# A hand-placed order of 820 operations replaced by another order of the same operations

## The chip, the cores and the metric

The kernel runs on one core of one Trainium2 chip. The time is the device time of one execution in microseconds; the median of three timed runs before the change is 188.65 us (188.63 to 188.68). One more execution was taken with the hardware profiler.

## What is computed

Two layers over 2048 steps and 640 channels, written side by side into one output of 2048 x 1280.

Half A is a diagonal state space layer with 640 complex states: `Bu = x B_bar^T`, then `h_t = Lam_bar h_{t-1} + Bu_t`, then `y = 2 Re(h C^T) + x * Dskip`, where `Lam_bar = exp(dt * Lam)` and `B_bar = (Lam_bar - 1)/Lam * B`.

Half B is a gated long convolution: `k` is convolved along time with four taps per channel, `kv = k_shift * v`, then `y = causal convolution of kv with a kernel of 2048 taps per channel + kv * ssm_D`, and the output is `q * y`. The reference does the long convolution by a Fourier transform of length 4096.

## The kernel before

The kernel is written as a list of operations. Each `P.add(name, engines, function, outs, ins, group)` appends one operation and gives it the next number; there are 820. `depend` works out from the memory that operations read and write which must come first. A group is a use of PSUM banks: its first operation (the products on TensorE) waits until the last user of those banks is done, and its last operation (the eviction) frees them.

Nothing is scheduled by a planner when the kernel is built. A string, `ORDER`, gives one token for each operation, such as `794T0`: the operation's number, its engine (V VectorE, A ScalarE, G GpSimd, T TensorE, S the SP queue for DMAs; a DMA can be issued on A too), and the first PSUM bank of its group (of eight). A small `t` is TensorE with the product cut in two column halves. `emit` walks through the string and issues each operation on the engine it names. So every engine runs its operations strictly in the string's order, the SP queue issues its DMAs strictly in that order, and the string also decides which engine does an operation that several can do, and which bank a product uses.

How the work is staged, in the order of time:

- Warm-up products, sine tables made by GpSimd (`wqh`, `gqh`, `sph`) and ScalarE (`w_s`, `g_s`), and a long chain of small VectorE operations on the 640 parameters (from `t_par`, `pv` to `fi`). B is loaded, turned on TensorE (`turn_B`) and evicted (`ev_B`).
- Half A upwards: `up2`, `up1`, `up0` join steps into blocks of 2, 4, 8 and 16 (line 588 holds the products with x, line 226 the others); `x` comes in eight transposing loads (`ld_x0` to `ld_x7`, line 554). Then `coarse` runs the recurrence over 128 blocks (`cs_...`), `gC` builds the output matrix, and `dn3` to `dn0` spread the states back to single steps (`ad`, line 735, adds on VectorE).
- Half B in two halves of 320 channels (`hf` 0 and 1): `s1h`, `s2h` transform the kernel, `conv` applies the four taps to five blocks of 128 channels (`cm`, `ca`, `cx`; line 832 loads k and v, and the k tile has one buffer), `plane` and `relay` re-arrange kv through DRAM, `s1k`, `s2k` transform kv, `product` multiplies the spectra (`pp`, `pq`, `py`, `pz`), `r2` and `r1` transform back (line 969 and 990 the products, 974 and 1008 or 1006 the evictions), `em1` multiplies by q when the eviction was done by ScalarE, and `store` writes.
- The output of half A, `project(i)` for 16 row sets: `ld_r` loads x rows (line 743, four buffers in turn), `xd` multiplies them by Dskip (line 744), `C` is the product (line 226 or 230), `ev_C` adds the two on VectorE (line 770) or only copies on ScalarE (line 768), in which case `em_C` adds (line 776), and `st_A` stores (line 780). Row set 13 is split into two halves, `C13_0` and `C13_1`, each with one bank; the others use two.

Numbers that matter below: 163, 162 and 168, 169 `ld_Braw`; 92 `t_par`, 93 `pv`, 109 `fi`; 170, 172 `turn_B1` and 171, 173 `ev_B1`; 220 `up21_0`, the first product with x, 222, 223 `up21_2` and its eviction; 177 `ld_x0`; 379, 390, 401, 445, 456 the five k loads; 195 and 209 the evictions `e1h0_2`, `e1h0_9`; 200 `s1h0_5`; 237 `ev_up0c_0`; 316 `r16`; 91 `ld_Dr` (Dskip to all partitions); 727, 728 `C0`, `ev_C0`; 732 `C1`; 744 `st_A3`; 504 `s2k0_30`, 505 `e2k0_30`; 699, 700 `r11_0`, `er11_0`; 702, 703 `r11_6`, `er11_6`; 705, 706 `r11_12`, `er11_12`; 720 `em11_28`; 708 to 711 and 721 to 724 the stores of half B's second half; 770, 771 `C8`, `ev_C8`; 808 `ld_r14`; 792 `ld_r12`, 793 `xd12`, 794 `C12`, 795 `ev_C12`; 809 `xd14`, 811 `ev_C14`; 816 `C15`, 817 `ev_C15`; 800, 801 `C13_0`, `ev_C13_0`; 804, 805 `C13_1`, `ev_C13_1`; 803, 807 their stores.

The loop that turns the string into instructions, and the place where it is read:

```python
for i, e, bank in order:
    o = self.ops[i]
    ...
    own = range(bank, bank + o.group.nb)
    if o is o.group.ops[0]:
        need |= {held[b] for b in own if held[b] is not None}
...
order = [(int(x[:-2]), x[-2].upper(), int(x[-1])) for x in ORDER.split()] if ORDER else plain_order(c.P)
c.P.narrow = {int(x[:-2]) for x in ORDER.split() if x[-2] == "t"}
```

Of the kernel before, what the change touches and what calls it, by code (L numbers as in the profile page):

```python
# [1115 lines left out]
def plain_order(P):  # L1116
# [19 lines left out]
    "169A0 157G0 162S0 0V0 58G0 6T0 17G0 168A0 163S0 110G0 19V0 148G0 87V0 11G0 18V0 89A0 90S0 12G0 3T1 42G0 13V0 88S0 183S0 "  # L1136
    "67G0 22V0 4T0 25V0 172T1 26G0 23V0 65V0 149G0 39V0 66V0 112G0 59V0 72G0 9T0 184S0 166T2 46G0 30G0 170T0 69G0 181S0 92T3 "
    "5T4 93V3 20V0 10T5 111G0 94A0 68G0 167A2 95V0 1T4 164T5 32V0 161G0 2T4 182S0 125V0 123V0 102V0 165A5 31V0 128V0 96V0 8T2 "
    "103V0 21V0 104V0 61V0 173A1 7T4 127V0 105V0 28V0 14V0 106V0 220T2 60V0 101A0 107V0 100A0 36V0 98A0 108V0 171A0 124V0 37V0 "
    "174S0 38V0 129V0 33V0 109V0 40V0 62V0 114G0 318V0 113G0 126V0 27V0 115G0 29V0 41V0 116G0 117G0 150G0 222T0 221A2 175S0 "  # L1140
    "118G0 43G0 97A0 99A0 119A0 44G0 212T2 156S0 63A0 121V0 152G0 379S0 71A0 223V0 15A0 47G0 70A0 210T0 213V2 153G0 45A0 120V0 "
    "50G0 122V0 179S0 214T2 132V0 144V0 211A0 52G0 147V0 160A0 188S0 74G0 180S0 218T0 130V0 382A0 51G0 131V0 48G0 34A0 228T4 "
    "381A0 77G0 187S0 186S0 54G0 215A2 383V0 216T6 73G0 219A0 133V0 158S0 384A0 229V4 82G0 238T0 83G0 185S0 134V0 217A6 35V0 "
    "55G0 135V0 49A0 380S0 262T6 385V0 56G0 386A0 78G0 254T4 79G0 53A0 387V0 390S0 151G0 75A0 226T2 263V6 239A0 177S0 255A4 "
    "84G0 189V0 57A0 178S0 388V0 202T4 155A0 196T6 246T0 203V4 197A6 391S0 392V0 227A2 393V0 137V0 394V0 192T2 247A0 230T6 "
    "270S0 193A2 395V0 396V0 76A0 154A0 224T2 397V0 145V0 231A6 401S0 136V0 146V0 142A0 64V0 204T0 398V0 225A2 190T6 240T4 81A0 "
    "399V0 389S0 402S0 205A0 141A0 191A6 200T0 404V0 194t2 16A0 139A0 232T6 138V0 24V0 195A2 403V0 272S0 405V0 143A0 201A0 80A0 "
    "406V0 198T0 407V0 241A4 248T2 199A0 408V0 400S0 233A6 409V0 86A0 445S0 242T4 249A2 316V0 206T0 243A4 250T2 140A0 207A0 "
    "410V0 234T6 412S0 251A2 244T4 208T0 235A6 176V0 245A4 411S0 252T2 236T6 256T4 253A2 416S0 209A0 237A6 85A0 321V0 159S0 "
    "317V0 448V0 302T6 447V0 257A4 314T0 303A6 319t2 258T4 320V2 315A0 310T6 449V0 415S0 259A4 312T2 311A6 417S0 260T4 300T0 "  # L1150
    "414S0 322V0 261A4 450V0 304T6 313A2 413S0 264T4 323V0 305A6 273S0 301A0 451V0 306T0 418S0 452V0 265A4 324t6 419S0 298T2 "
    "307A0 325V6 266T4 446S0 299A2 274T0 267V4 282T6 326V0 268T4 275A0 286T2 283V6 269A4 308T0 287A2 327V0 328t6 296T4 330V0 "
    "309A0 276T2 329V6 297A4 294T0 277V2 725S0 424t6 456S0 295A0 331V0 280T4 337T2 332V0 281A4 432T0 425A6 335V0 333T4 338A2 "
    "278T6 334V4 271S0 433A0 288T2 279V6 434T4 289A2 336V0 426T0 730S0 453V0 435A4 339t6 441S0 442S0 420T2 427A0 340V6 422T4 "
# [93 lines left out]
```

## Time and profile before

| | us |
|---|---|
| median of three runs (188.63 to 188.68) | 188.65 |
| the profiled execution | 187.94 |
| its span, first to last instruction | 186.2 |
| TensorE busy | 175.9 (94%) |
| VectorE busy | 157.2 (84%) |
| ScalarE busy | 147.4 (79%) |
| GpSimd busy | 72.1 (39%) |

Times in the profile count from the span's start. In a row of a timeline the first number is the start, the second how long it took, then the engine, the line of the kernel, the operation, what it writes and reads, the shapes, the number of instructions merged into the row, and in brackets how long the engine sat idle before and what ended that. `SPq` rows are the time that the SP queue took to issue a DMA, not the transfer. In the table of stretches, each engine's busy time is followed by its number of instructions, then come the granted TensorE clock, the mean busy share of the DMA engines and GB/s. In a row of a group the numbers after the bar are busy us and the mean of one in ns, after the second bar the idle time before. Matmuls are pipelined and their ends are modelled, so neighbouring rows overlap a little.

### The profile page before, as it was taken

The numbers are of one execution on the slowest core, as the hardware profiler recorded it, in microseconds if no ns is written. First come the engines' busy times: TensorE is split into PE (matmuls) and PEld (weight loads), VectorE is DVE, ScalarE is ACT, GpSimd is POOL, SyncE is SP. The second block draws the span as 40 slices with busy tenths as digits, with TensorE's granted clock in tenths as the row PEclk, the third lists the DMA queues.
The fourth block names the chain that finished last, engine by engine and source line by source line (L and its number), as shares of the span: only waits on it lengthen the run. The fifth ranks groups of instructions, "written<-read, shape, count | busy, mean of one in ns | idle before, by whom it ended". The sixth has DMA issues, their size and how long they took to land.

```text
span 186.2 us, 7668 instructions
## 1 busy us (share of the span) xinstructions
PE 175.9 (94%) x3398; PEld 121.9 (65%) x3399; DVE 157.2 (84%) x227; ACT 147.4 (79%) x181; POOL 72.1 (39%) x68
## 2 busy tenths in 40 slices
PE   7999999999999989889989999999999999999991
PEld 3554555455668766566676588776578876887770
DVE  3538767799659899999979989899999999998971
ACT  2369797999999999999997988997898874984000
POOL 8669999900000000016804924820830000541620
PEclk9999999999999999999999999999999999999999
DMA  5999999899999989999999579302496993058995
GB/s 156 189 180 166 202 152 129 165 171 212 192 239 248 232 145 161 181 167 145 141 108 273 182 151 132 49 5 75 142 186 129 223 209 76 25 158 189 230 212 154
DMA packets 106826, 30.15 MB, mean 162 GB/s; under 512 B 101290, under 2 KB 106154, under 8 KB 106794
## 3 DMA queue, kind: packets, MB, share of 16 engines
q1 hardware_dynamic: 106476, 29.35, 87.5%
q8 instruction: 26, 0.43, 1.1%
q10 hardware_dynamic: 318, 0.33, 0.6%
q14 instruction: 6, 0.05, 0.1%
HBM read 11.32 MB, written 7.86 MB: 103 GB/s over the span
## 4 chain that ended last, share of the span: by engine, by line
PE 39%; DVE 20%; DMA 13%; POOL 11%; SPq 7%; ACT 5%; issue 3%; DVEq 0%; POOLq 0%; ACTq 0%
PE acc L226 17%; DMA arena<-in_B_k_dram 6%; PE acc L918 6%; PE acc L230 5%; SPq L825 4%; DVE arena L206 4%; DVE arena L735 4%; POOL arena L310 4%; PE acc L969 3%; DMA arena<-in_A_Dskip_dram 3%; DMA arena<-in_B_ssm_k_dram 3%; PE acc L990 3%; DVE arena L858 3%; ACT arena L931 2%; ACT arena L974 2%
## 5 line engine op out<-in xcount | busy, mean ns | idle before, releaser
L588 PE MATMUL acc<-arena 128*64 128x512 bf16 x400 | 45.4, 380 | 0.5 <-DVE arena L605 0.3
L931 ACT CAST arena<-acc 128x960 bf16<-128x960 f32 (+1 forms) x43 | 37.4, 916 | 4.0 <-PE acc L918 2.1
L226 PE MATMUL acc<-arena 128*128 128x320 bf16 (+2 forms) x255 | 36.4, 298 | 2.2 <-DVE arena L770 1.0
L904 ACT CAST arena<-acc 128x1024 bf16<-128x1024 f32 x37 | 35.8, 1037 | 1.2 <-PE acc L899 1.2
L588 PEld LDWEIGHTS <-arena 128*64 128x64 bf16 x400 | 22.2, 110 | 20.1 <-DVE arena L605 0.8
L226 PEld LDWEIGHTS <-arena 128*128 128x128 bf16 x256 | 23.7, 98 | 12.0 <-DVE arena L770 1.2
L859 POOL TENSOR_TENSOR arena<-arena 128x2048 bf16<-128x2048 bf16 x2 | 8.5, 4274 | 53.0 <-DVE arena L858 45.2
L918 PE MATMUL acc<-arena 128*64 128x160 bf16 x512 | 23.6, 235 | 1.0 <-DVE arena L686 0.6
L230 PE MATMUL acc<-arena 128*64 128x320 bf16 (+3 forms) x258 | 23.2, 313 | 0.7 <-DVE arena L697 0.5
L918 PEld LDWEIGHTS <-arena 128*64 128x64 bf16 x512 | 18.6, 110 | 7.6 <-ACT arena L931 2.2
L858 DVE TENSOR_TENSOR arena<-arena 128x2048 bf16<-128x2048 bf16 x14 | 17.8, 1269 | 4.7 <-ACT arena L207 4.5
L735 DVE TENSOR_TENSOR arena<-acc,arena 128x1024 bf16<-128x1024 f32 (+2 forms) x19 | 20.4, 1115 | 0.9 <-PE acc L230 0.5
L776 POOL TENSOR_TENSOR arena<-arena 128x640 bf16<-128x640 f32 x3 | 4.2, 1417 | 32.6 <-ACT arena L768 32.6
L974 ACT CAST arena<-acc 128x1024 bf16<-128x1024 f32 x16 | 15.4, 1026 | 1.7 <-PE acc L969 1.5
L230 PEld LDWEIGHTS <-arena 128*64 128x64 bf16 x258 | 12.9, 110 | 3.8 <-DVE arena L697 0.6
L206 DVE TENSOR_SCALAR arena<-arena 128x2048 bf16<-128x2048 bf16 x15 | 11.0, 749 | 4.9 <-DMA arena<-in_B_k_dram 4.7
L894 PE MATMUL acc<-arena 128*64 128x128 bf16 x400 | 14.6, 221 | 0.5 <-ACT arena L605 0.3
L894 PEld LDWEIGHTS <-arena 128*64 128x64 bf16 x400 | 12.5, 110 | 3.4 <-ACT arena L904 0.9
L770 DVE TENSOR_TENSOR arena<-acc,arena 128x640 bf16<-128x640 f32 (+1 forms) x14 | 10.8, 774 | 3.0 <-PE acc L226 2.5
L207 ACT ACTIVATE arena<-arena 128x2048 bf16<-128x2048 bf16 (+2 forms) x10 | 11.1, 1111 | 1.9 <-DVE arena L858 1.1
L942 DVE TENSOR_TENSOR arena<-arena 128x2560 bf16<-128x2560 bf16 x8 | 11.9, 1485 | 0.1
L609 PE MATMUL acc<-arena 128*64 128x256 bf16 (+2 forms) x140 | 11.4, 291 | 0.2 <-ACT arena L655 0.2
(142 smaller groups left out, 283.0 us busy)
## 6 DMA issues: line engine op xcount, KB each, us to landing
out_dram<-arena SPq DMA_DIRECT2D x31, 160.0 KB, 3.4
arena<-in_B_ssm_k_dram SPq DMA_DIRECT2D x8, 320.0 KB, 5.9
kv_rows<-arena SPq DMA_DIRECT2D x5, 512.0 KB, 4.5
arena<-kv_rows SPq DMA_DIRECT2D x16, 160.0 KB, 4.0
arena<-in_A_x_dram SPq DMA_DIRECT2D x16, 160.0 KB, 3.4
arena<-in_B_q_dram SPq DMA_DIRECT2D x8, 320.0 KB, 6.1
arena<-in_A_B_im_dram ACTq DMA_DIRECT2D x1, 160.0 KB, 3.0
arena<-in_A_B_re_dram SPq DMA_DIRECT2D x1, 160.0 KB, 2.8
```

Source lines behind the costliest of these rows:

```text
L206: vm = lambda e: lambda out, in_, by: e.tensor_scalar_mul(out=out, in0=in_, scalar1=by)
L226: e.matmul(out, lhsT=lhsT, rhs=rhs, start=start, stop=stop, skip_group_check=True)
L230: e.matmul(out[half], lhsT=lhsT[:, half], rhs=rhs, start=start, stop=stop, skip_group_check=True, tile_position=(0, 64 * r))
L588: e.matmul(o[64 * r:64 * r + 64], lhsT=self.BT[j][:, r, d, :], rhs=self.XP[:, d, 2 * q:2 * q + 2], start=(d == 0), stop=(d == 4), skip_gro ...
L735: e.tensor_tensor(out=o, in0=b, in1=o, op=ALU.add)
L858: P.add(f"ca{d}_{j}", tt, lambda e: e.tensor_tensor(out=t1, in0=t1, in1=t2, op=ALU.add), outs=[t1], ins=[t1, t2])
L894: e.matmul(B[64 * b:64 * b + 64, 128 * i:128 * i + 128], lhsT=lh[i], rhs=F[:, b, :], start=True, stop=True, tile_position=(0, 64 * b))
L904: P.add(f"e1{what}{hf}_{u}", {PACT: act(1024), PDVE: dve(1024)}, lambda e, B: c.CP[e](out=out, in_=(B.rearrange("p (l n s k) -> p k s l n" ...
L918: e.matmul(B[64 * s:64 * s + 64, 512 * b + 160 * i:512 * b + 160 * i + 160], lhsT=c.W[:, k, 64 * b:64 * b + 64], rhs=self.AS[hf][:, k, 160 ...
L931: c.CP[e](out=out, in_=b.rearrange("p r (k j n) -> p r k j n", k=n, j=4) if nj > 1 else b.rearrange("p r (k x) -> p r k x", k=n))
L942: P.add(f"pp{hf}", n1, lambda e: e.tensor_tensor(out=pt, in0=X, in1=Yk, op=ALU.mult), outs=[pt], ins=[X, Yk])
L974: P.add(f"er2{hf}_{u}", {PACT: act(1024), PDVE: dve(1024)}, lambda e, B: c.CP[e](out=out, in_=B.rearrange("p (s n b) -> p b s n", s=2, n=4 ...
```

## The change

Only the string `ORDER` changes. It has the same 820 numbers; the functions, the shapes and the number of products cut in halves (40) stay. Tokens move, 61 of them name another engine, and many name another bank. Of the operations that can run on several engines, VectorE has 242 tokens instead of 231, ScalarE 173 instead of 182, GpSimd 72 instead of 74. (An `em` token makes no instruction when its eviction is on VectorE.) The lines that are spoken of below:

```diff
 ORDER = (
...
-    "67G0 22V0 4T0 25V0 172T1 26G0 23V0 65V0 149G0 39V0 66V0 112G0 59V0 72G0 9T0 184S0 166T2 46G0 30G0 170T0 69G0 181S0 92T3 "
-    "5T4 93V3 20V0 10T5 111G0 94A0 68G0 167A2 95V0 1T4 164T5 32V0 161G0 2T4 182S0 125V0 123V0 102V0 165A5 31V0 128V0 96V0 8T2 "
-    "103V0 21V0 104V0 61V0 173A1 7T4 127V0 105V0 28V0 14V0 106V0 220T2 60V0 101A0 107V0 100A0 36V0 98A0 108V0 171A0 124V0 37V0 "
...
-    "118G0 43G0 97A0 99A0 119A0 44G0 212T2 156S0 63A0 121V0 152G0 379S0 71A0 223V0 15A0 47G0 70A0 210T0 213V2 153G0 45A0 120V0 "
...
-    "55G0 135V0 49A0 380S0 262T6 385V0 56G0 386A0 78G0 254T4 79G0 53A0 387V0 390S0 151G0 75A0 226T2 263V6 239A0 177S0 255A4 "
...
-    "439A2 459V0 440S0 345t6 458V0 352A4 284T0 502T2 346V6 460G0 285A0 349t4 503A2 91S0 467T0 350V4 353t6 468A0 292T2 354V6 "
...
-    "569V0 769V0 571S0 699T0 771V6 772V0 705T2 700A0 702T4 773S0 712T6 572S0 701V0 810T0 713A6 579S0 706V2 707G0 570S0 573S0 "
-    "714G0 703V4 704G0 815V0 708S0 816T4 792S0 809G0 709S0 799V0 710S0 811V0 812G0 718T2 715T6 793G0 813S0 719V2 720V0 794T0 "
-    "711S0 716V6 717G0 817V4 818V0 723S0 721S0 724S0 800T4 795V0 796G0 819S0 722S0 797S0 804T0 801V4 802G0 803S0 805V0 806G0 "
-    "807S0"
...
+    "112G0 61V0 26G0 22V0 21V0 67G0 126V0 10T1 46G0 183S0 166T0 72G0 92T1 7T2 93V1 128V0 94A0 113G0 125V0 15A0 30G0 95V0 157G0 "
+    "127V0 172T1 28V0 102V0 181S0 96V0 103V0 39V0 98A0 164T2 124V0 97A0 38V0 65V0 100A0 101A0 104V0 6T3 167A0 105V0 37V0 106V0 "
+    "36V0 3T4 107V0 14V0 165A2 108V0 109V0 9T0 32V0 40V0 114G0 66V0 182S0 99A0 41V0 111G0 1T4 59V0 115G0 60V0 110G0 25V0 173V1 "
+    "69G0 4T0 129V0 170T1 220T4 31V0 116G0 171V1 73G0 175S0 130V0 68G0 62V0 117G0 222T0 131V0 149G0 221V4 118G0 174S0 148G0 "
+    "47G0 27V0 150G0 212T4 156S0 48G0 379S0 54G0 49A0 210T2 56G0 119A0 121V0 152G0 120V0 177S0 42G0 218T6 33V0 211A2 29V0 44G0 "
+    "213V4 223A0 179S0 55G0 160V0 63A0 228T0 34A0 82G0 382A0 35V0 144V0 180S0 74G0 122V0 224T4 70A0 151G0 229V0 185S0 188S0 "
...
+    "241A4 134V0 204T6 195V0 316G0 242T4 205A6 202T2 403V0 81A0 200T0 404V0 232T6 201A0 402S0 405V0 203A2 406V0 80A0 407V0 "
+    "248T2 85A0 389S0 408V0 137V0 409V0 243A4 445S0 233A6 208T0 249A2 317V0 244T4 136V0 234T6 209V0 245A4 138A0 143A0 139A0 "
+    "250T2 235A6 140A0 410V0 141A0 206T4 251A2 236T6 252T2 207A4 256T0 413S0 237V6 142V0 411S0 176V0 253A2 86A0 91S0 321V0 "
...
+    "680A6 798S0 573S0 577S0 718T6 771V0 772G0 702T4 799G0 719A6 705T2 773S0 699T0 578S0 810T6 700V0 701G0 579S0 580S0 706V2 "
+    "707V0 808S0 720V0 703V4 704V0 712T2 715T0 815V0 708S0 794T4 716V0 717G0 710S0 792S0 709S0 713V2 714G0 809G0 722S0 816T2 "
+    "711S0 723S0 793V0 724S0 795V4 796V0 811V6 812V0 797S0 800T4 817V2 818V0 813S0 721S0 804T2 801V4 802V0 803S0 819S0 805V2 "
+    "806V0 807S0"
 )
```

59 rows, old and new, of the table ORDER are left out of this document.

## The prediction

> **What bounds the kernel now.** I read the page first (shares, slices), then a table of busy time in six stretches, then the timelines of TensorE, VectorE, the SP queue and GpSimd at the places where the new list differs. The one profiled execution took 187.94 us, 1.74 more than its span, and lies 0.71 under the median 188.65 of the three timed runs; differences are worked out inside the span and added to that median.
>
> ```profile
> span 186.2 us, 7668 instructions
> PE 175.9 (94%) x3398; PEld 121.9 (65%) x3399; DVE 157.2 (84%) x227; ACT 147.4 (79%) x181; POOL 72.1 (39%) x68
> ```
>
> ```profile
> core 0: us, PE busy (x) PEld busy (x) DVE busy (x) ACT busy (x) POOL busy (x), PEclk, DMA share, GB/s
> 0.00:9.46 9.46, 8.39 (x42) 4.07 (x43) 4.51 (x34) 3.27 (x6) 7.00 (x23) 1.00 0.83 174
> 9.46:37.40 27.94, 27.57 (x253) 14.13 (x252) 19.46 (x37) 23.94 (x31) 26.50 (x28) 1.00 1.19 166
> 37.40:66.30 28.90, 27.67 (x454) 19.00 (x455) 23.85 (x33) 27.93 (x41) 0.28 (x1) 1.00 1.10 217
> 66.30:98.10 31.80, 29.04 (x725) 20.98 (x726) 30.13 (x39) 31.08 (x38) 8.14 (x2) 1.00 1.04 144
> 98.10:165.90 67.80, 66.72 (x1573) 51.75 (x1574) 65.34 (x72) 57.36 (x66) 25.16 (x12) 1.00 0.65 133
> 165.90:182.40 16.50, 16.49 (x358) 11.94 (x356) 13.39 (x17) 3.84 (x4) 4.99 (x3) 1.00 0.89 211
> ```
>
> TensorE sets the pace. Between its first real product at 9.46 and its last at 182.4 it is idle 5.45 us (0.37, 1.23, 2.76, 1.08, 0.01). Both lists hold the same products in nearly the same sequence and as many narrow ones (40), so TensorE's own work does not change; a new order can win at most those 5.45 us, and can lose any amount. Half of it lies between 66.3 and 98.1, where VectorE (30.13 of 31.80) and ScalarE (31.08) are both full, and there the wins must be found. The DMA share is at 1.0 until 98: until then a transfer that moves up pushes others back.
>
> **The front, up to 66 us.** Three edits matter.
>
> ```profile
> 9.46 6.67 PE L588 MATMUL acc<-arena 128*64 128x512 bf16 x60
> 16.46 3.86 PE L588 MATMUL acc<-arena 128*64 128x512 bf16 x34 [0.34 <-DVE arena L605]
> 6.50 0.19 DVE L379 COPY arena<-acc 128x30 f32<-128x30 f32 x1 [3.13 <-PE acc L377]
> 10.18 0.17 DVE L399 CAST arena<-arena 128x10 int32<-128x10 f32 x1
> ```
>
> (1) Eviction 173 (ev_B1) goes from ScalarE to VectorE, into bank 1 and behind the whole chain of small parameter operations, which in the kernel before runs from 6.50 (pv) to the end of 10.18 (fi), 3.8 us. The last turn (170) needs that bank and stands directly ahead of the first product (220). t_par moves up past one turn, so the chain starts about 1.2 us earlier, at 5.3, and has 20 operations where it had 27 (0.1 each by the spacing of these rows): fi ends near 8.4. Eight more small ones, 0.8 of eviction (128x640 from PSUM, the row 97.26 below) and the turn's 0.4 give 10.1 to 10.4, less what the chain's own waits may save. I take 10.1: +0.6, bounds -0.1 and +1.4. (2) Eviction 223 leaves VectorE for ScalarE, which takes away the 0.34 before 16.46. Left over: +0.3.
>
> ```profile
> 34.53 2.11 SPq L832 DMA_TRANSPOSE arena<-in_B_k_dram  x1
> 36.68 3.50 SPq L554 DMA_TRANSPOSE arena<-in_A_x_dram  x2
> 46.69 2.18 SPq L832 DMA_TRANSPOSE arena<-in_B_k_dram  x1
> 39.82 1.40 DVE L206 TENSOR_SCALAR arena<-arena 128x2048 bf16<-128x2048 bf16 x2
> ```
>
> (3) On the SP queue ld_x0 (half of the 3.50, 1.75) moves from behind the second k load to ahead of ld_x2. Everything between moves back 1.75: k1 is issued at 36.3, its first taps start at 41.5 instead of 39.82, and VectorE's conv 1 ends as much later. Behind conv 1 on VectorE now stands eviction 195 (e1h0_2, moved there from ScalarE), and the product s1h0_5 (200) waits for the bank that it frees: TensorE is up to 1.2 us late near 52, and all later products queue behind that wait. The third k load is not moved, since x0 has been issued by then: 46.69, or at most 0.4 later.
>
> **From 53 to the product C1 at 98.** What is late there is VectorE, not TensorE.
>
> ```profile
> 53.39 0.75 DVE L206 TENSOR_SCALAR arena<-arena 128x2048 bf16<-128x2048 bf16 x1 [4.00 <-DMA arena<-in_B_k_dram]
> 60.21 0.82 DVE L673 COPY arena<-arena 128x1280 f32<-128x1280 f32 x1
> 95.09 0.53 DVE L827 TENSOR_TENSOR arena<-arena 128x80 bf16<-128x80 bf16 x1 [0.21 <-DMA arena<-in_B_ssm_k_dram]
> 96.64 0.49 DVE L744 TENSOR_TENSOR arena<-arena 128x640 bf16<-128x640 bf16 x1 [1.02 <-DMA arena<-in_A_Dskip_dram]
> 97.26 0.82 DVE L770 TENSOR_TENSOR arena<-acc,arena 128x640 bf16<-128x640 f32 x1
> 53.39:98.09 44.70, 41.18 (x935) 30.42 (x932) 42.12 (x56) 43.52 (x59) 8.14 (x2) 1.00 1.04 169
> 98.14 0.58 PE L226 MATMUL acc<-arena 128*128 128x320 bf16 x3 [0.88 <-DVE arena L770]
> ```
>
> From the landing of the third k to the end of ev_C0 (98.08) VectorE works 42.12 of 44.70 us, and C1 starts when it is done. So what TensorE loses ahead of this, up to about 1 us, is absorbed and counts 0; it is priced as 1.5 in rival (c). In this stretch the new list adds to VectorE e1h0_9 (1.22, a 1024-column eviction as in the row 166.06 below) and an ev_up0c (about 0.4), takes r16 (0.82, to GpSimd, which has nothing else there) and a cf (0.16): +0.6. The Dskip load (ld_Dr) goes up past all the relay loads and the h loads, so the 1.02 before 96.64 goes: -1.0, but the next limits stand close behind: TensorE's own work up to C0, and ScalarE (43.52 of 44.70), which must now also do e2k0_30 (8/12 of the 0.98 below) before C1: +0.4. Sum 0 at C1, bounds -1.2 and +1.2.
>
> **98 to 166.** TensorE is idle 1.08 in 67.8.
>
> ```profile
> 166.06 1.22 DVE L974 CAST arena<-acc 128x1024 bf16<-128x1024 f32 x1
> L974 ACT CAST arena<-acc 128x1024 bf16<-128x1024 f32 x16 | 15.4, 1026 | 1.7 <-PE acc L969 1.5
> L931 ACT CAST arena<-acc 128x960 bf16<-128x960 f32 x33 | 31.1, 978 | 2.0 <-ACT arena L931 0.9 <-PE acc L918 0.3 <-DVE arena L744 0.3
> ```
>
> VectorE gives up three er21 (3.7), ev_C9 and a pz0 (0.8 each), two em10 (1.1) and three xd (1.4), and takes two er21 (2.4), ev_C5, ev_C11 and em_C10 (0.8 each), er10_0 (1.15) and one xd (0.5): 7.8 against 6.5, 1.3 less. ScalarE takes the three er21 (1.03 each) and ev_C9 (0.7) and gives up two er21, two ev_C and er10_0: 0.6 less. Two pq0 change places between VectorE and GpSimd one for one. Three relay loads now stand behind st_A3, which waits for ev_C3 near 112.3; they are issued by 115, when the last one is in the kernel before, so s1k1 is not late. I take -0.2, bounds -1.1 and +1.0.
>
> **The end.** Here I see a new wait.
>
> ```profile
> 168.86 0.82 DVE L770 TENSOR_TENSOR arena<-acc,arena 128x640 bf16<-128x640 f32 x1 [0.21 <-PE acc L226]
> 168.70 1.77 PE L990 MATMUL acc<-arena 64*64 64x80 bf16 x176
> 170.94 1.88 DVE L1008 TENSOR_TENSOR arena<-acc,arena 128x640 bf16<-128x640 f32 x2
> 165.66 0.48 DVE L1013 TENSOR_TENSOR arena<-arena 128x640 bf16<-128x640 bf16 x1
> 172.73 1.21 SPq L1024 DMA_DIRECT2D out_dram<-arena  x2
> 174.04 0.47 SPq L743 DMA_DIRECT2D arena<-in_A_x_dram  x1
> 178.11 1.39 POOL L744 TENSOR_TENSOR arena<-arena 128x640 bf16<-128x640 bf16 x1 [2.95 <-DMA arena<-in_A_x_dram]
> 173.82 1.68 DVE L744 TENSOR_TENSOR arena<-arena 128x640 bf16<-128x640 bf16 x1
> 173.51 1.65 POOL L744 TENSOR_TENSOR arena<-arena 128x640 bf16<-128x640 bf16 x1
> 179.78 0.82 DVE L770 TENSOR_TENSOR arena<-acc,arena 128x640 bf16<-128x640 f32 x1 [0.69 <-PE acc L226]
> 181.07 0.49 DVE L770 TENSOR_TENSOR arena<-acc,arena 128x320 bf16<-128x320 f32 x1 [0.46 <-PE acc L226]
> 182.43 0.49 DVE L770 TENSOR_TENSOR arena<-acc,arena 128x320 bf16<-128x320 f32 x1 [0.87 <-PE acc L226]
> arena<-in_A_x_dram SPq DMA_DIRECT2D x16, 160.0 KB, 3.4
> ```
>
> ld_r12 (792) is issued at 174.04 and xd12 can start 4.07 later, at 178.11; that is 0.3 in time for ev_C12 at 179.78, and nobody waits, since C13_0 takes the banks of C15, not of C12. In the new list ld_r12 stands behind stores 708 and 710, and 708 waits for er11_6, on VectorE behind er11_0 (moved there from ScalarE), er11_12 and em11_28. er11_0's product is now the last of four: done at 168.70 + 1.77 = 170.5. Then VectorE has er11_0 (1.15), er11_12 and er11_6 (the 1.88 of row 170.94 together) and em11_28 (0.48): 3.5 in all, and er11_6 ends at 174.0. Two stores at 0.6 and ld_r12 is issued at 175.2, +1.2. With the 3.4 that such loads have in the median it lands at 178.6, with its own 4.07 at 179.3. xd12 is now on VectorE (0.48), so ev_C12 ends at 179.9 to 180.6; in the kernel before it ends at 180.6 (179.78 + 0.82). But in the new list C13_0 takes bank 4, C12's own, and C13_1 takes bank 2, C15's; on VectorE ev_C14 and ev_C15 are queued behind the waiting xd12 and ev_C12, 0.74 each, so C13_1 may start at 181.4 to 182.1. In the kernel before the rows 181.07 and 182.43, 1.36 apart, put its start at about 181.0. So +0.4 to +1.1 from the load alone; two stores go out just ahead of it, so I take the upper part, +1.0, bounds 0 (landing within 3.0) and +1.8. The last store follows after that as in the kernel before.
>
> The two rows at 173.5 show VectorE's xd13 at 1.68 while GpSimd's xd14 ran 1.65; alone it takes 0.48. [...]
>
> **Sum.** What the front loses (+0.3, and up to +1.2 at the bank of e1h0_2) is absorbed between 53 and 98 and counts 0; the stretch up to C1 counts 0; the stretch 98 to 166 counts -0.2; the end counts +1.0. That is +0.8 in all: 188.65 + 0.8 = 189.45, said as 189.5.
>
> **Rivals.** (a) The load of Dskip is what the new order is worth: the 1.02 and the 0.21 ahead of C1 go, ScalarE has room after all, and ld_r12 lands within 3.0 us: -1.2, 187.4. For it: the rows 96.64 and 98.14 name that load alone; against it: VectorE's +0.6 and the full ScalarE. It decides from the point where ev_C0 is ready before C0 ends. (b) Same operations, same time: the idle is only moved about, the load is in time: 188.65. For it: the 5.45 us are spread over dozens of small bank waits. (c) The front is not absorbed: the 1.75 of conv 1 also holds up the third k load by its single buffer, and 1.5 reach C1 on top of the end's 1.0: 191.0. Against it: 46.69 leaves 1.4 after the last tap in the kernel before.
>
> **Chances.** Forecast 0.43, (a) 0.30, (b) 0.17, (c) 0.10. The measurement tells 0.2% (0.38 us) from nothing; a few hundredths of the forecast fall into that band, and about as many of (b) to the fast side: slower 0.50, same 0.18, faster 0.32. The cases (a) and (c) are the ends of the range, 187.3 to 191.0; the forecast's own range is 188.9 to 190.3.
>
> **What would show it.** The first L588 product at 10.1 (9.4 to 10.9). C1's first L226 product within 1 us of 98.1 with no Dskip wait on VectorE. At the end a VectorE wait at L744 for in_A_x_dram of about 3 us, released near 179, and a TensorE gap at L226 of 0.4 to 1.2 released by VectorE L770. If that L744 operation waits for nothing, or if C1 comes at 97 or sooner, the prediction is wrong.

## The result: slower, and by more than forecast

| | median, us | runs | lowest to highest |
|---|---|---|---|
| kernel before | 188.63 | 7 | 187.21 to 189.22 |
| kernel after | 191.68 | 7 | 189.83 to 194.75 |

The ratio is 1.0148, with a 95% interval of 1.0108 to 1.0187: 2.8 us slower (2.0 to 3.5). The forecast was +0.8 us, in a range that ended at 191.0. The sign was right; the time lies outside the range. The ratios here leave disturbed executions out, which the lowest and highest times hold.

The profiled execution of the kernel after took 192.18 us with a span of 190.4, where that of the kernel before had 186.2. So 4.2 us have to be found in this pair of traces, more than the 2.8 of the medians. One execution is not the median, and what differs from one execution to the next comes out below.

### The profile page after: what moved, and what is told of

The parts are those of the page before. It is cut to its first block, busy times and chain, and to the rows that moved or that the text cites. A ratio compares the mean times of both kernels' runs of the same rounds, so it can differ in the third digit from the quotient of the medians.

```text
span 190.4 us, 7669 instructions
## 1 busy us (share of the span) xinstructions
PE 176.2 (93%) x3396; PEld 121.2 (64%) x3396; DVE 160.5 (84%) x231; ACT 140.2 (74%) x172; POOL 75.6 (40%) x70
## 4 chain that ended last, share of the span: by engine, by line
PE 40%; DVE 20%; SPq 17%; ACT 8%; DMA 6%; issue 6%; POOL 0%; DVEq 0%; ACTq 0%; POOLq 0%
PE acc L226 16%; PE acc L918 7%; DVE arena L735 7%; PE acc L230 7%; SPq L554 6%; DMA arena<-in_B_k_dram 6%; SPq L825 4%; DVE arena L858 3%; ACT arena L904 3%; DVE arena L206 3%; PE acc L969 3%; PE acc L990 3%; SPq L832 3%; SPq L519 3%; PE acc L588 2%
## 5 line engine op out<-in xcount | busy, mean ns | idle before, releaser
L588 PE MATMUL acc<-arena 128*64 128x512 bf16 x400 | 44.9, 379 | 0.0
L230 PE MATMUL acc<-arena 128*64 128x320 bf16 (+2 forms) x252 | 23.3, 318 | 0.1
L770 DVE TENSOR_TENSOR arena<-acc,arena 128x640 bf16<-128x640 f32 (+1 forms) x15 | 11.5, 777 | 4.7 <-PE acc L226 4.0
L744 POOL TENSOR_TENSOR arena<-arena 128x640 bf16<-128x640 bf16 x7 | 9.8, 1400 | 13.5 <-DMA arena<-in_A_x_dram 13.5
L206 DVE TENSOR_SCALAR arena<-arena 128x2048 bf16<-128x2048 bf16 (+1 forms) x17 | 12.4, 750 | 2.4 <-DMA arena<-in_B_k_dram 2.2
L969 PE MATMUL acc<-arena 64*128 64x128 bf16 x320 | 11.4, 224 | 1.1 <-issue 1.1
L1013 POOL TENSOR_TENSOR arena<-arena 128x640 bf16<-128x640 bf16 (+1 forms) x2 | 3.4, 1722 | 22.3 <-ACT arena L1006 22.3
```

The costliest lines, as they stand in the source:

```text
L206: vm = lambda e: lambda out, in_, by: e.tensor_scalar_mul(out=out, in0=in_, scalar1=by)
L230: e.matmul(out[half], lhsT=lhsT[:, half], rhs=rhs, start=start, stop=stop, skip_group_check=True, tile_position=(0, 64 * r))
L588: e.matmul(o[64 * r:64 * r + 64], lhsT=self.BT[j][:, r, d, :], rhs=self.XP[:, d, 2 * q:2 * q + 2], start=(d == 0), stop=(d == 4), skip_gro ...
L969: e.matmul(B[:, 512 * s + 128 * i:512 * s + 128 * i + 128], lhsT=lh[i][s][r], rhs=rh, start=(r == 0), stop=(r == 1), tile_position=(64 * s ...
```

## The profile after

First the page of the kernel after: its first lines, and the shares of the chain that ended last (the kernel before had "issue 3%" there).

```profile
span 190.4 us, 7669 instructions
PE 176.2 (93%) x3396; PEld 121.2 (64%) x3396; DVE 160.5 (84%) x231; ACT 140.2 (74%) x172; POOL 75.6 (40%) x70
...
PE 40%; DVE 20%; SPq 17%; ACT 8%; DMA 6%; issue 6%; POOL 0%; DVEq 0%; ACTq 0%; POOLq 0%
```

TensorE works nearly as long as before (176.2 against 175.9), so nearly all of the loss is idle time. The same six stretches of the kernel after show where it lies:

```profile
0.00:9.46 9.46, 7.16 (x36) 2.90 (x36) 5.06 (x41) 4.26 (x11) 5.92 (x23) 1.00 0.83 167
9.46:37.40 27.94, 27.52 (x257) 14.46 (x259) 20.48 (x29) 19.94 (x21) 26.97 (x29) 1.00 1.14 172
37.40:66.30 28.90, 26.66 (x436) 18.04 (x434) 26.23 (x37) 23.96 (x35) 1.55 (x1) 1.00 1.10 209
66.30:98.10 31.80, 30.10 (x659) 21.33 (x653) 30.38 (x40) 31.13 (x40) 9.48 (x3) 1.00 1.07 161
98.10:165.90 67.80, 65.26 (x1606) 50.27 (x1602) 63.93 (x70) 56.17 (x64) 28.88 (x13) 1.00 0.59 124
165.90:182.40 16.50, 15.04 (x396) 11.50 (x393) 10.69 (x14) 4.76 (x6) 2.79 (x2) 1.00 0.68 169
```

TensorE's idle time, stretch minus its busy time, before and after: 0.37 and 0.42; 1.23 and 2.24; 2.76 and 1.70; 1.08 and 2.54; 0.01 and 1.46. The middle moved as foreseen: one lost near 52, one won back ahead of 98. The last two stretches, in which I had expected -0.2 and, at one place near the end, +1.0, lost 2.9.

The waits of TensorE name what the page calls "issue", time in which the engine waited for nothing that the profile shows. The columns are line, what was waited for, us in total, how often, and the longest:

```profile
PE acc L990 <- issue: 1.4, 3, 1.0
...
PE acc L969 <- issue: 1.1, 1, 1.1
```

A third row of this kind, of 0.98 at line 377 (`t_par`, at 5.59), lies in the warm-up ahead of a product's only instruction; it isn't one of those meant here and comes up again under the front. The kernel before has no such row for TensorE. The timeline of the kernel after shows the four one by one:

```profile
162.14 0.79 PE L990 MATMUL acc<-arena 64*64 64x80 bf16 x65
163.96 0.48 PE L990 MATMUL acc<-arena 64*64 64x80 bf16 x31 [1.03 <-issue]
164.37 3.36 PE L969 MATMUL acc<-arena 64*128 64x128 bf16 x97
168.79 0.71 PE L969 MATMUL acc<-arena 64*128 64x128 bf16 x15 [1.05 <-issue]
169.43 0.85 PE L226 MATMUL acc<-arena 128*128 128x320 bf16 x5
...
173.51 0.80 PE L990 MATMUL acc<-arena 64*64 64x80 bf16 x68 [0.24 <-issue]
174.24 2.89 PE L226 MATMUL acc<-arena 128*128 128x320 bf16 x20
177.07 0.55 PE L990 MATMUL acc<-arena 64*64 64x80 bf16 x40
177.78 0.70 PE L990 MATMUL acc<-arena 64*64 64x80 bf16 x56 [0.17 <-issue]
178.41 8.42 PE L226 MATMUL acc<-arena 128*128 128x320 bf16 x60
```

Each of these pieces falls in the middle of a product: r10_16 (48 matmuls) stops after 17 of its own, r21_0 (16 matmuls) after one. A wait for a bank or for data stands ahead of a product's first instruction. So what is late here isn't data. The stretches from one such piece to the next, with the instructions of TensorE counted (matmuls, then weight loads):

```profile
163.95:168.77 4.82, 3.77 (x128) 3.54 (x128) 4.22 (x6) 3.82 (x5) 1.91 (x2) 1.00 0.60 139
168.77:173.50 4.73, 4.48 (x127) 3.37 (x128) 1.80 (x2) 1.89 (x3) 0.02 (x1) 1.00 0.67 175
173.50:177.77 4.27, 4.11 (x128) 3.01 (x128) 3.41 (x5) 0.00 (x0) 1.37 (x1) 1.00 0.71 166
```

128 and 128 (one matmul's record is missing in the second row): the pieces lie 256 instructions apart. The page's part on DMA queues has "q8 instruction: 26, 0.43", 26 packets of 16 KB. TensorE has 6,792 matmuls and weight loads, 26.5 times 256. My theory from here on: TensorE gets its instructions in blocks of 256, one packet each, and the pieces are waits for the next block. It has to stand against two rivals: that the waits belong to these products or to the transfers beside them, and that they were one execution's accident.

## Experiments

**1 and 2. The same two lists, shifted by 126 instructions.** If blocks are what counts, it must be possible to move the waits without touching the order. One warm-up product of 512 columns is replaced by 64 small ones, whose results nobody reads.

```diff
-            for _ in range(2):
+            for _ in range(1 if k == 0 else 2):
                 e.matmul(B[:, 0:512], lhsT=z[:, 0:128], ...)
+            for m in range(64 if k == 0 else 0):
+                f = 64 * (m & 1)
+                e.matmul(B[f:f + 64, 0:80], lhsT=z[0:64, 0:64], ..., tile_position=(0, f))
```

> The kernel after, but the first warm-up product is one of 512 columns and 64 small ones of 80 instead of two of 512: 126 more TensorE instructions ahead of everything, at about the same time. Theory (instruction supply): TensorE's four idle pieces at the end that nothing in the profile explains (1.03, 1.05, 0.24 and 0.17 us) lie exactly 256 instructions apart, so they are waits for the next block of instructions; with 126 more ahead the block ends fall on other products, the pieces at r10_16 and r21_0 go or move by 126 instructions, and the time is 189.8 to 191.0. Rival (the waits belong to the order, that is to these products, their data or the transfers beside them): the same two pieces of about 1 us at the same products, 191.7.

> The kernel before with the same 126 more TensorE instructions ahead. Theory (instruction supply): the kernel before has no such wait because its block ends happen to lie well; shifted by 126, one falls into the row of small products r11_0, r11_12, r11_6, r11_16 behind C8, and a wait of 0.5 to 1.5 us appears there or nearby that names no releaser: 189.1 to 190.1. Rival (the waits belong to the new order): nothing changes, 188.6, and no such wait.

Measured: after, shifted 1.0363 (1.0319 to 1.0406) of the kernel before; before, shifted 1.0229 (1.018 to 1.0277). The functions' lines lie four further down in these two files (r1 is L994, r2 is L973). The timeline of TensorE, the kernel after, shifted:

```profile
155.85 0.55 PE L994 MATMUL acc<-arena 64*64 64x80 bf16 x38 [0.60 <-issue]
166.84 2.64 PE L973 MATMUL acc<-arena 64*128 64x128 bf16 x78 [1.01 <-issue]
176.03 0.23 PE L994 MATMUL acc<-arena 64*64 64x80 bf16 x3 [2.00 <-issue]
```

and the kernel before, shifted:

```profile
155.13 0.58 PE L994 MATMUL acc<-arena 64*64 64x80 bf16 x41 [1.17 <-issue]
174.28 0.61 PE L994 MATMUL acc<-arena 64*64 64x80 bf16 x22 [2.27 <-issue]
```

The kernel before, which had no such wait, gets two of them, 3.4 us together, from nothing but 126 instructions ahead. In the kernel after they leave their places and turn up at others. Counted from TensorE's first instruction, the pieces shown begin at 5,537, 6,048 and 6,559 and at 5,536 and 6,558; those of the kernel after at 5,794, 6,050, 6,305 and 6,561. Divided by 256 all nine leave 158 to 162 (a few records are missing in each trace): one grid of 256. One more, of 0.79 at 126.41 in the kernel after, shifted, begins at 4,258 (remainder 162), in the middle of a product with C: it isn't only the short products that have them. Both shifted kernels have 27 packets of 16 KB instead of 26. So the waits belong to the place in the instruction stream, and not to the products. My numbers for the times were far too low: I had 189.8 to 191.0 for the first kernel and at most 190.1 for the second, and 1.0363 and 1.0229 are 194.7 and 192.2 on the scale of 187.9 that was measured for the kernel before in that comparison. Not all of the second is instruction waits. The small products start its first real product at 10.85 where it was 9.46. And in its profiled execution the granted clock is 0.54 in the 3.7 us behind the wait of 2.27, so that 40 products take 7.00 there, where they take 5.61 elsewhere:

```profile
174.82 7.00 PE L226 MATMUL acc<-arena 128*128 128x320 bf16 x40
```

The size of the waits I could not forecast.

**3. Shifted by 256.** Nine warm-up steps each have one of their two products replaced by 15 small ones (one by 17).

> The kernel after with 256 more TensorE instructions ahead: in nine warm-up steps one of the two products of 512 columns becomes 15 (once 17) small ones of 80 columns, which take about as long. Theory (blocks of 256 instructions): a shift by one whole block puts the block ends on the same products as in the kernel after, so the pieces of about 1 us without a releaser are back in r10_16 and r21_0, where the shift by 126 had none. Rival (any more instructions, or another start, move them): they lie elsewhere or are gone. The time itself is not compared, 190 to 193.

```profile
168.07 0.48 PE L994 MATMUL acc<-arena 64*64 64x80 bf16 x31 [0.75 <-issue]
168.49 3.37 PE L973 MATMUL acc<-arena 64*128 64x128 bf16 x97
172.08 0.71 PE L973 MATMUL acc<-arena 64*128 64x128 bf16 x15 [0.23 <-issue]
```

31, 97 and 15 matmuls: matmul for matmul the places of the kernel after. Its own time, 195.92 in one run, contains a late start (the first real product at 15.05, behind the small ones) and is not compared. That the places come back after 256 instructions is shown.

**4. The dense products ahead of r21_1.** r10_22 and r10_16 have 96 instructions each and take 0.5 us each (1.05 for both in the kernel before). In the kernel before they stand straight behind C11; in the kernel after three r2 products stand between.

```diff
-788T6 660V0 783A2 568A0 663V0 569G0 556V4 557V0 681T0 789V6 790G0 563G0 689T4 682A0 695T2 791S0 690V4 564T6 696A2 558T0 ...
+788T6 660V0 783A2 568A0 663V0 569G0 564T2 556V4 557V0 558T0 565A2 789V6 790G0 559V0 560V0 563G0 681T4 689T6 682A4 695T2 ...
```

Their evictions (565, 559) and 560 move up with them.

> The kernel after, with r10_22 and r10_16 (96 instructions each in 0.6 us) placed straight behind C11, ahead of r21_1, as in the kernel before, and the banks behind them renamed to fit. Theory (instruction supply): r21_1 waits for pz1, and in the new list these two dense products come behind that wait; ahead of it they are fed while C11 runs. The pieces of 1.03 and 1.05 go: 191.7 - 2 = 189.7 (to 190.3 if the small ones at r11 stay). Rival (transfers, or the products themselves): at most the 0.1 us wait changes, 191.7.

Measured: 1.0056 (1.0021 to 1.009) of the kernel before. From 1.0148 that is 0.92%, 1.7 us, the largest single part of the loss. Its timeline of TensorE has no piece named "issue" any more at the end, but a larger wait that was hidden until then:

```profile
158.98 1.05 PE L990 MATMUL acc<-arena 64*64 64x80 bf16 x96
159.97 5.43 PE L969 MATMUL acc<-arena 64*128 64x128 bf16 x160
165.53 2.89 PE L226 MATMUL acc<-arena 128*128 128x320 bf16 x20
168.35 1.71 PE L990 MATMUL acc<-arena 64*64 64x80 bf16 x160
...
180.20 2.99 PE L226 MATMUL acc<-arena 128*128 128x320 bf16 x20 [0.74 <-DVE arena L770]
```

That last row is C13_0 and C13_1, waiting for VectorE's ev_C12: the late load of my prediction, below.

**5. The front of the one, the end of the other.** The list after up to C10, then all that is left in the order and the banks of the list before.

> The list of the kernel after up to and with C10, then everything that is left in the order, on the engines and in the banks of the kernel before. Theory: what is lost ahead of C10 (1.1 us by the two profiles) stays, and the unexplained waits behind C11 go: 189.7 to 190.0. Rival (my predicted late load at the end is what costs, or a front that is absorbed): 188.6 to 188.9. Rival (the loss is all in the front and in chance): 191 or more.

Measured: 1.0073 (1.0035 to 1.0111), 188.99 beside 187.9: 1.1 to 1.4 us over the kernel before, and behind C11 no unexplained wait, as expected. But the reason that I had given for the number, 1.1 us lost ahead of C10, isn't in its trace: C10 starts at 153.55, in the kernel before at 153.62. What its trace loses is the seam, where TensorE waits 0.43 ahead of r10_16 and 0.29 ahead of the first r2. So that the number came out as expected is luck, and a fixed loss ahead of C10 isn't shown.

**6. The late load.** ld_r12 moved ahead of the stores 708 and 710, in the kernel of experiment 4 and in the kernel after.

```diff
-... 808S0 720V0 703V4 704V0 712T2 715T0 815V0 708S0 794T4 716V0 717G0 710S0 792S0 709S0 ...
+... 808S0 792S0 720V0 703V4 704V0 712T2 715T0 815V0 708S0 794T4 716V0 717G0 710S0 709S0 ...
```

> The kernel with r10_22 and r10_16 ahead of r21_1, and in addition ld_r12 (792) on the SP queue behind ld_r14, ahead of the stores 708 and 710. Theory (the late load that I predicted): TensorE's wait of 0.73 ahead of C13_0, which came to light when the instruction waits were gone, goes: 1.0056 falls by 0.7 to 0.9 us, to 1.001 (0.998 to 1.004) of the kernel before. Rival (the wait is the two banks and VectorE's queue, or the DMA engines are full there and the load only swaps places with stores): 1.004 to 1.007.

> The kernel after with one edit: ld_r12 (792) behind ld_r14, ahead of the stores 708 and 710. Theory (the late load is hidden behind the instruction waits): in the kernel after TensorE waited only 0.08 for ev_C15, since it was itself 4 us late, so nothing is gained: 1.012 to 1.018 of the kernel before, and the waits without a releaser are still there. Rival (the late load costs its 0.4 to 0.9 us here too): 1.010 or less.

Measured: with experiment 4 1.0034 (0.9998 to 1.007), in the kernel after alone 1.0103 (1.007 to 1.0136). In the first, TensorE's wait for VectorE at the end is gone; its last products run in one piece:

```profile
173.40 8.37 PE L226 MATMUL acc<-arena 128*128 128x320 bf16 x60
```

The ratio falls by 0.22%, 0.4 us, half of what I expected, and within the two intervals. In the kernel after alone the ratio fell by 0.45%, 0.8 us, where I had expected nothing, though its interval overlaps that of the kernel after. Its trace has smaller instruction waits (0.48 and 0.23) and still 0.21 ahead of C13_0. The picture of "hidden behind the other" is thus too simple: how much of the load shows depends on how late TensorE is in that execution. What the load alone costs in the kernel after is not settled by these runs; 0 to 0.8 us.

**7. The front.** Experiments 4 and 6, and ld_x0 back behind the second k load and e1h0_2 back on ScalarE.

```diff
-... 120V0 177S0 42G0 ...   390S0 64V0 ...         ... 204T6 195V0 316G0 ...
+... 120V0 42G0 ...         390S0 177S0 64V0 ...   ... 204T6 195A0 316G0 ...
```

> The same, and in the front the load of x0 (177) back behind the second k load, and the eviction e1h0_2 (195) back on ScalarE, as in the kernel before. TensorE's wait of 1.46 ahead of s1h0_5 near 52 goes. Theory (the front is absorbed, as I predicted: between 53 and 98 something else sets the time): the same as without this edit, within 0.3 us. Rival (TensorE's front is carried to C1, since the Dskip wait is gone): 1.0 to 1.4 us less, 0.993 to 0.996 of the kernel before.

Measured: 1.0055 (1.0019 to 1.009) where it was 1.0034 without the edit. TensorE's wait near 52 is gone, and nothing is gained. In the profiled execution another wait stands ahead of C1, on VectorE and then on TensorE:

```profile
97.92 0.52 DVE L827 TENSOR_TENSOR arena<-arena 128x80 bf16<-128x80 bf16 x1 [1.98 <-DMA arena<-in_B_ssm_k_dram]
```
```profile
98.50 0.71 PE L899 MATMUL acc<-arena 64*64 64x64 bf16 x64 [1.58 <-DVE arena L827]
99.15 1.12 PE L226 MATMUL acc<-arena 128*128 128x320 bf16 x7
```

L827 is addD1, which waits for the last of four h loads; s1h1_5 (L899) waits for addD1, and C1 stands behind s1h1_5.

**8 and 9. The Dskip load in the kernel before.** First its load alone is moved (91 behind the store 411, ahead of the relay loads). Then also TensorE's and VectorE's order around C1, so that nothing there waits for the h loads, and ld_r12 ahead of 708.

```diff
-... 727t2 462V0 501A4 481A0 444V0 726V0 603S0 463A0 525t0 728V2 533t4 523t6 731V0 732T2 729S0 455S0 526A0 464V0 740S0 534A4 473V0 465G0 524A6 504T4 733V2 367t0 505A4 482T6 ...
+... 727t2 462V0 501A4 481A0 726V0 504T4 603S0 463A0 728V2 732T6 731V0 505A4 444V0 525t0 533t4 523t2 729S0 455S0 526A0 464V0 740S0 534A4 473V0 465G0 733V6 524A2 482T6 367t0 ...
```

> The kernel before with one edit: the load of Dskip (91) goes up behind the store 411, ahead of the relay loads, as in the new list. The wait of 1.02 on VectorE ahead of xd0 goes in any case. Theory (the load alone held C1): C1 starts 0.7 to 0.9 earlier and the time is 187.8, 0.995 to 0.996. Rival (my sum: what stands close behind takes the wait's place): within 0.2 us of the kernel before.

> The kernel before with three edits: the Dskip load (91) early, behind the store 411; around C1 the product s2k0_30 and then C1 directly behind C0, C1 in bank 6 that is free (s1h1_4 in bank 2 instead), s1h1_5, s1h1_9 and s1h1_4 behind C1, and on VectorE xd0 and ev_C0 ahead of addD1, which waits for the h loads; and ld_r12 ahead of store 708. Theory (with the Dskip load early, the h loads through addD1 and s1h1_5 were what held C1): C1 starts at 96.5 to 97.0 with s2k0_30 already done, no wait takes its place, and the time is 0.993 to 0.996 of the kernel before. Rival (ScalarE, full in this stretch, or a later use of the h products takes it back): 0.998 to 1.002.

Measured: 1.0051 (1.0021 to 1.0081) and 1.0125 (1.0096 to 1.0154), both slower than the kernel before. In the first, the Dskip wait is gone and addD1's stands in its place on VectorE; TensorE waits longer than it did for Dskip (0.88). The h loads also land later in this execution: addD1 starts at 96.46, in the kernel before at 95.09. Why they do is not shown.

```profile
96.46 0.53 DVE L827 TENSOR_TENSOR arena<-arena 128x80 bf16<-128x80 bf16 x1 [2.34 <-DMA arena<-in_B_ssm_k_dram]
```
```profile
97.08 1.10 PE L899 MATMUL acc<-arena 64*64 64x64 bf16 x96 [1.51 <-DVE arena L827]
```

In the second, C1 starts at 96.49 instead of 98.14, as expected. Behind it TensorE waits at two places:

```profile
96.49 2.89 PE L226 MATMUL acc<-arena 128*128 128x320 bf16 x20
...
101.27 0.47 PE L918 MATMUL acc<-arena 128*64 128x160 bf16 x8 [0.96 <-DVE arena L770]
...
102.72 0.64 PE L894 MATMUL acc<-arena 128*64 128x128 bf16 x16 [0.55 <-ACT arena L904]
```

The first wait is my own order (ev_C1 behind two long VectorE operations). The second is ScalarE, which had stood idle for 1.65 us, since s1h1_5, s1h1_9 and s1h1_4 came later, and then had their three evictions at once. Of the 2.1 us that this trace's span is longer, 0.7 are there when TensorE's last product ends (183.09 against 182.39); the other 1.4 lie behind it, in the last stores. Three edits at once were too many to say what each is worth.

**10. Is it the wait for pz1 that delays the block?** r21_1 waits for the last pz1. On TensorE's sequence nothing is changed; pq1 660 goes to GpSimd and up, pz1 663 ahead of py1 673.

```diff
-... 641V0 538A2 787V0 670V0 ... 672V0 782T2 671V0 673V0 674V0 781V0 788T6 660V0 783A2 568A0 663V0 ...
+... 641V0 538A2 660G0 670V0 ... 672V0 782T2 671V0 663V0 673V0 674V0 781V0 787V0 788T6 783A2 568A0 ...
```

> The kernel after with TensorE's sequence and banks untouched; ahead of r21_1, pq1 660 goes from VectorE to GpSimd and up (2.6 us there by the kernel before, whose own time there is idle), pz1 663 goes ahead of py1 673, and xd11 behind xd10, so that the last pz1 that r21_1 needs ends near 158.2 instead of 159.9. In the kernel after the block of instructions for the end of r10_16 was fetched 1.2 us behind the end of that pz1. Theory (the wait for pz1 holds up the instruction stream, and the fetch with it): the fetch comes 1.5 us or more sooner, the two pieces of about 1 us shrink below 0.3, and the time is 1.004 to 1.010 of the kernel before. Rival (the dense products r10_22 and r10_16 at that place are enough by themselves): the pieces stay, as in the repeated kernel after.

Measured: 1.0247 (1.021 to 1.0283). The profiled execution, at 194.99, was the longest of the six; the others took 191.2 to 193.07. The edit did the opposite of what it was for. GpSimd's pq1 took 3.20, and VectorE's py1 beside it 3.12 instead of 0.82; the last pz1 ended at 162.0, not 158.2. The two rows, VectorE and GpSimd:

```profile
151.65 3.12 DVE L947 TENSOR_TENSOR arena<-arena 128x1280 bf16<-128x1280 bf16 x1
```
```profile
150.89 3.20 POOL L945 TENSOR_TENSOR arena<-arena 128x1280 bf16<-128x1280 bf16 x1 [12.38 <-DVE arena L942]
```

py1 starts 0.76 behind pq1 and ends 0.68 after it: 3.12 beside GpSimd's operation, 2.3 us more than the 0.82 of the same operation at 147.71 and 160.47 of this trace. The rows at 173.5 of the kernel before are another such pair: VectorE's xd13 took 1.68 beside GpSimd's 1.65, where the median of its line on VectorE is 0.48. What holds VectorE up in such a pair these traces don't show.

TensorE then waited 2.39 ahead of r21_1, for an eviction on ScalarE, and its granted clock fell behind that: 0.56 in this stretch, which begins 1.15 us after the wait.

```profile
163.85 1.78 PE L969 MATMUL acc<-arena 64*128 64x128 bf16 x48 [2.39 <-ACT arena L1006]
```
```profile
165.00:168.00 3.00, 3.00 (x130) 2.78 (x126) 1.74 (x2) 2.54 (x3) 3.00 (x3) 0.56 0.18 60
```

The other five executions have a mean granted clock of 0.987 to 0.991, the kernel after beside them (experiment 11) 0.998 to 1.0. By an estimate from these clocks, one per cent of 190 is up to 1.9 us, about the whole difference between 1.0247 and the 1.0153 of experiment 11. So this ratio can't be read as the price of the wait alone. An instruction wait (0.86, at 129.52, instruction 4,260, remainder 164) is in this trace too, while the two at r10_16 and r21_0 are gone, perhaps because TensorE came there late and at a lower clock.

The question itself got an answer from the trace all the same. From each trace I took the start of the 16 KB packet that by my theory brings the block on whose first instruction r10_16 stops (5,794), in the kernel after the last one ahead of that stop, and the end of the last pz1 (in the shifted kernels it is the block that begins at 6,050 and at 5,793):

| kernel | what follows C11 | last pz1 ends | packet starts | later by |
|---|---|---|---|---|
| after | r21_1 | 159.88 | 161.07 | 1.19 |
| after, second time | r21_1 | 159.31 | 160.49 | 1.18 |
| ld_r12 early (6) | r21_1 | 159.22 | 160.39 | 1.17 |
| pq1 on GpSimd (10) | r21_1 | 162.02 | 163.21 | 1.19 |
| shifted by 256 (3) | r21_1 | 164.27 | 165.46 | 1.19 |
| shifted by 126 (1) | r21_1, 126 instructions further on in its block | 160.67 | 158.18 | -2.49 |
| r10 first (4) | r10_22 | 158.59 | 156.96 | -1.63 |
| r10 first, ld_r12 early (6) | r10_22 | 158.19 | 156.26 | -1.93 |
| after to C10, then before (5) | r10_22 | 160.91 | 157.34 | -3.57 |
| experiment 7 | r10_22 | 159.93 | 158.04 | -1.89 |

Where r21_1 is next and stands about 30 instructions into its block, the packet starts 1.17 to 1.19 after the pz1 for which r21_1 waits, in five traces of five. In four of them (all but that of experiment 10) TensorE itself doesn't stand still then: it is busy with C11. The first instruction of the block runs 2.35 to 2.89 after the packet starts, in the four in which TensorE then had to wait for it. Where r10_22 is next, or r21_1 stands further on in the block, the packet comes before that pz1 ends. So the end of pz1 alone doesn't set the packet's start; the place of the wait in the block counts too. My reading is that the supply of instructions stands at the wait for pz1, and that the packet follows when that wait is over. No trace shows the supply itself, so this is an estimate from the times of the table; in experiment 10 the packet even starts 0.64 before r21_1 runs (163.85), which had its ScalarE eviction to wait for as well.

**11. The kernel after once more.**

> The kernel after, unchanged, a second time, beside the run above. Theory: 1.010 to 1.019 of the kernel before, with the pieces without a releaser again in r10_16 and r21_0, and of a size that may differ from one execution to another. Rival (they were one execution's accident): none of them, or at other products.

Measured: 1.0153 (1.0112 to 1.0193). The first two pieces are back in the same places, smaller; the two small ones behind them are not:

```profile
162.84 0.48 PE L990 MATMUL acc<-arena 64*64 64x80 bf16 x31 [0.47 <-issue]
...
166.84 0.71 PE L969 MATMUL acc<-arena 64*128 64x128 bf16 x15 [0.22 <-issue]
...
181.59 2.99 PE L226 MATMUL acc<-arena 128*128 128x320 bf16 x20 [0.23 <-DVE arena L770]
```

The places are fixed, the sizes are not. The packet took 0.93 here and 1.38 in the first execution, and the first instruction came 2.35 and 2.89 after its start.

**From C10 on.** From each trace I took the start of C10 and the end of TensorE's last product. The products between are the same in all.

| kernel | C10 starts | last product ends | between |
|---|---|---|---|
| before | 153.62 | 182.39 | 28.77 |
| after | 154.73 | 186.83 | 32.10 |
| after, second time | 154.17 | 184.58 | 30.41 |
| ld_r12 early (6) | 154.07 | 184.65 | 30.58 |
| r10 first (4) | 153.44 | 183.19 | 29.75 |
| r10 first, ld_r12 early (6) | 153.04 | 181.77 | 28.73 |
| after to C10, then before (5) | 153.55 | 183.03 | 29.48 |

The last six have the same list up to C10, and reach it from 0.6 sooner to 1.1 later than the kernel before: there is no fixed price on that side. From C10 on the new list takes 1.6 to 3.3 longer, and with r10_22 and r10_16 first and ld_r12 early as long as the old one. Each row is one execution.

No kernel of these was faster than the kernel before. The best is experiment 6 with 1.0034, which may be no difference.

## Why the prediction was right in sign and wrong in size

**The front, right in mechanism, the number partly luck.** The first product starts at 10.27 in the profiled execution (10.1 forecast), with the last turn held for eviction 173 as described. But `t_par` came late there, behind the wait of 0.98 that the page calls "issue", and the eviction took 0.48 where I had 0.8. Six other executions of the same front, without that wait, have the first product at 9.47 to 9.66. Experiments 8 and 9, with the front of the kernel before, have it at 8.96 and 8.93, so against those the step is again 0.5 to 0.7. At s1h0_5 TensorE waits 1.41 for e1h0_2 on VectorE, where I had up to 1.2:

```profile
52.88 0.64 PE L894 MATMUL acc<-arena 128*64 128x128 bf16 x16 [1.41 <-DVE arena L904]
```

**53 to 98, right in sum, the reason only in part.** C1 starts at 98.91 (98.14 before) in the profiled execution, and at 97.28 to 99.31 in six other traces that have the same front, from 0.9 sooner to 1.2 later: 0 within bounds of 1.2, as I took it. The Dskip wait is gone. I named VectorE's extra 0.6 us and ScalarE as what takes its place. Experiments 7 and 8 showed a nearer one that I had quoted and passed over: the 0.21 ahead of addD1, whose h loads land at 95 to 98. Moving Dskip alone puts a longer wait there and makes the kernel before slower. That holds only where TensorE comes early. In the profiled execution of the kernel after neither VectorE nor TensorE waits for the h loads (addD1 starts at 97.27), and of the seven traces with its front TensorE does so in one (experiment 6 without experiment 4, 1.43). So the h loads are a limit close behind that I had passed over; what absorbs the front where TensorE comes late is not shown, and in the profiled execution nothing does: first product 0.81 later, C1 0.77 later.

**98 to 166 and on to the end, wrong.** I put -0.2 up to 166, with bounds of -1.1 and +1.0, and behind it only the late load. The failed step stands at the start of the prediction: both lists hold the same products, "so TensorE's own work does not change". Its busy time didn't (176.2 against 175.9), but I took from this that TensorE waits for banks and data only, and put waits for its instructions at nothing without a reason. In the profiled execution they are 2.5 us, 1.0 of it ahead of 166 and 1.5 behind; in the ratios, from the kernel after to experiment 4, 1.7 us. Added to the forecast of 0.8 that makes 2.5, near the 2.8 measured, but this sum is partly luck: the 0.8 was to come from the late load, which isn't settled in the kernel after. Experiment 4 leaves 1.0056, 1.1 us; 0.4 of it goes with the early load, within the intervals, and the cause of the rest stays open. In the kernel before no product waits without a releaser; in the kernel after four waits of 0.17 to 1.05 us stand behind C10, and in the kernels shifted by 126 such waits are up to 2.27.

What could have raised the question: in the kernel before, TensorE runs r10_22, r10_16 and ten r2 products between two C products without a gap.

```profile
159.45 1.05 PE L990 MATMUL acc<-arena 64*64 64x80 bf16 x96
160.44 5.50 PE L969 MATMUL acc<-arena 64*128 64x128 bf16 x160
```

In the new list the first r2 comes ahead of the two r10. In neither does TensorE wait for data there, but only the second puts 192 instructions that take 1.05 us behind a wait for VectorE. Where the block ends would fall could not be read off the list without counting.

**The end, right in mechanism, not shown in size.** xd12 waits on VectorE for ld_r12, and ev_C12, ev_C14 and ev_C15 are queued behind it as described:

```profile
182.36 0.49 DVE L744 TENSOR_TENSOR arena<-arena 128x640 bf16<-128x640 bf16 x1 [1.61 <-DMA arena<-in_A_x_dram]
182.95 2.29 DVE L770 TENSOR_TENSOR arena<-acc,arena 128x640 bf16<-128x640 f32 x3
```

The load goes out at 178.69, since er11_6 and the stores ahead of it are late with TensorE. ev_C15 ends at 185.24 and C13_1 starts at 185.30, when TensorE comes there by itself, so in that execution the wait costs 0.1. With the instruction waits out of the way (experiment 4) VectorE waits 2.53 for the load, up to 178.72, near the 3 us and the 179 that I had named, and TensorE 0.74, within the 0.4 to 1.1 of the prediction; but in the time it is 0.4, and with intervals that overlap.

**The rivals.** (a) fell: Dskip's wait did go, and no gain came of it. (b) fell. (c) named a loss of 2.3 us, near the measured one, for a wrong reason: the third k load went out only 0.7 later (47.38) in the profiled execution and 0.2 in the second, and the front did not reach C1 as a rule.

## What to carry to other kernels

TensorE stood idle here at places that are fixed in its instruction count, 256 apart, for 0.17 to 1.05 us in the kernel after and up to 2.27 in the shifted ones. Where products have many short instructions (here 96 in 0.5 us), a wait ahead of them that TensorE doesn't feel, since it is busy with older work, can cost all the same: with r10_22 and r10_16 ahead of that wait the ratio fell from 1.0148 to 1.0056. The loss turned up later, in the middle of a product and with no releaser; that the wait holds up the supply of instructions is my estimate from the times in the table of experiment 10. Pieces without a releaser at equal distances in the instruction count are the mark of it (the name "issue" alone isn't: `t_par` had it too), and adding a few instructions far ahead is a cheap proof. A load that comes out of the critical chain is worth nothing until the next arrival has been looked up; the idle time in brackets of the very next row, however small, is the place to look. And before a ratio is put down to a wait, the granted clock of its runs has to be compared (here 0.987 to 0.991 in experiment 10, 0.998 to 1.0 in the kernel after beside it).

## What the runs showed of the hardware that I had not expected

- Beside its 6,792 TensorE instructions the kernel after has 26 packets of 16 KB on the queue q8, and nine pieces without a releaser, in three traces, lie on one grid of 256 instructions (remainders 158 to 162). Most places of this grid cost nothing that the profile shows; in the kernel after four of 26 cost 0.17 to 1.05 us, in the kernel before none, in the shifted kernels the longest 2.27. With 126 more instructions ahead of everything the kernel before took 2.3% longer; its trace has 3.4 us of such waits beside the later start (1.4) and the products at a lower clock (1.4).
- The packet in the table of experiment 10 started 1.17 to 1.19 us after the end of the VectorE operation for which r21_1, about 30 instructions into the block before, waited, in five traces of five. In the kernel after the packets ahead of the four pieces start at 161.07, 166.54, 171.08 and 175.38, and TensorE goes on 2.89, 2.25, 2.43 and 2.40 after them. Whether the transfers beside it lengthen this was not tried; in the kernel after, the DMA engines moved 0.15 MB in the 4.7 us ahead of the packet at 161.07, so crowding did not make that one late.
- In the two traces in which TensorE stood idle for over 2.2 us in its dense last part (2.27 and 2.39), the granted clock fell: it was 0.54 in the 3.7 us behind the wait of 2.27, and 0.56 in the 3.0 us that begin 1.15 after the wait of 2.39. In the kernel after, shifted by 126, with idle pieces of 2.00 and 1.81, the mean clock of the execution is 0.998, and behind the 2.00 it runs 20 products in 2.89, as it does elsewhere. That the idle time is the cause was not tried.
- Where an order's waits fall on this grid changed with an edit far ahead of them: the kernel before got two (1.17 and 2.27) with 126 more instructions of TensorE, and the kernel after had the first two of its own in the same places (0.75 and 0.23) with 256 more.
